# An attention and maxout FFN kernel: token tiles of 256 and 384 in place of 384 alone

## The chip, the core and the metric

The kernel runs on one core of one Trainium2 chip. The metric is the device time of one execution in microseconds (us). A core has five engines that run side by side, each through its own queue in order: PE (matrix multiply; its weight loads are shown apart as PEld), DVE (vector), ACT (activation), POOL (GpSimd) and SP, which here only issues DMAs. PE writes to PSUM banks; ACT and DVE read them, POOL can't.

## What is computed

Eight batches with eight heads, 576 tokens and 64 numbers per head. Half of the heads attend to the last 32 tokens, half to every fourth of the last 128. The result, turned to 4608 tokens of 512 numbers, goes through an FFN whose hidden layer is the elementwise largest of three products.

```python
scores = scale * np.matmul(q, k.transpose(0, 1, 3, 2))
mask_plain = (rel >= 0) & (rel < window)
mask_dil = (rel >= 0) & (rel < window * dilation) & (rel % dilation == 0)
...
attn = attn / (np.sum(attn, axis=-1, keepdims=True) + 1e-09)
return np.matmul(attn, v).astype(np.float32)
...
h = np.maximum(np.maximum(x @ w1, x @ w2), x @ w3)
return (h @ w_out).astype(np.float32)
```

## The kernel before

**Units.** The attention is cut into 64 units: a unit is half of a batch's tokens (288, the constant HALF) for two heads, and four units make one half (NPAIR). The first twelve units (LEAN) are written by dense (L490): scores s (L498 to L530, on PE with a mask added by a matmul), the largest value and the exponentials (DVE, ACT), the sums, the division W (norm, L595, mostly on POOL), transposes pt on PE, copies PT by ACT or DVE, and the product with the values, pv (L612). The other 52 are written by attention and behind (L650, L683), which turn W with transposes of DVE instead of PE. At the end of each unit, rounded (L638) writes the sum xH, a rounded part, and xL, the rest, into a ring of 1152 tokens (RING, four halves).

**Weights.** Each of the 36 weight pieces (24 of the three up matrices, 12 of the down matrix) is loaded as 64-bit floating-point numbers and made into two 32-bit parts by a chain in weight (L382): two first steps (rebias on ACT, low3 on POOL), two integer steps on DVE (joined, sign), the high part (split, wupH or wdn) on ACT, and the low part (wupL or wdn) on POOL. Four up pieces c serve one of the six column groups f (NF); two down pieces serve one wdn tile.

**FFN.** ffn (L803) takes a tile of n tokens that starts at token t0. For each of the six f and each of the three matrices g, twelve matmuls of n columns (three terms of four, L815) gather in one of two PSUM banks (the tag ffn in BANKS); DVE or ACT takes the bank out into tmp, ACT rounds it to h, POOL subtracts for the low part of h. Then, for each 128 tokens of the tile, 18 matmuls of 512 columns (down, L870) make a block d of the output, which ACT copies to o and SP sends away. A chain named prev keeps all FFN matmuls in the order in which the program lists them: all u of a tile, all d of it, then the next tile.

**What a tile asks for.** In the loop at L930 a tile of n tokens from t0 may begin when every half with a token below t0 + n is there:

```python
halves = range(t0 // HALF, -(-(t0 + n) // HALF))
...
*(x_of[h, p][xz] for h in halves for p in range(NPAIR)),
*(w_of[4 * f + c][wz] for c in range(4)),
```

**Order.** Nothing is issued as it is listed. A planner (class Plan, L96) holds all steps with estimated costs per engine, gives each a goal and a due time that is worked back from the FFN's matmuls (deadlines, L122), and goes through time, taking at each point the step that can begin first (order, L157). Steps with several possible engines may spill to another one. Before the first FFN matmul, it puts filler matmuls (idle, L951) into PE's gaps, and a run of 16 where its clock passes 21 and 35 us (BURSTS). The order is thus fixed when the program is built, and each engine works through its queue in that order and waits where something is missing.

Of the kernel before, what the change touches and what calls it, by code (L numbers as in the profile page):

```python
# [25 lines left out]
NEG = -8e9  # L26
REBIAS = 2.0**-112
TICK = 10.24 / 3
TILES = [384] * 12


LEAN = 12
# [235 lines left out]
def tile_dilated_window_attention__then__maxout_ffn(  # L268
# [660 lines left out]
    u = t0 = 0  # L929
    for n in TILES:  # L930
        plan.kind = "a"
# [81 lines left out]
```

## Time and profile before

| | |
|---|---|
| median of 3 runs | 736.94 us (736.81 to 736.97) |
| span of the profiled execution, first to last instruction | 734.8 us |
| busy PE, weight loads, DVE, ACT, POOL | 721.2, 661.3, 379.7, 305.4, 237.3 us |
| granted clock of PE, mean | 0.999 |
| first FFN matmul; first d matmul | 49.15; 100.72 us |
| filler matmuls | 72, all before 49.15 us |

The profile is that of one execution; its time outside the span isn't shown, and the median stands 2.1 us above the span. A view of groups gives, for each line and shape, the count, the busy time, the mean duration of one, and the idle time of the engine ahead of it with what ended it. The chain of waits follows back from the last instruction to what released each step. A busy PE is not PE at its peak: matmuls overlap, so the pace is read from how long a run of them lasts, divided by their count.

### The profile page before, as it was taken

What the parts mean: (1) busy time and instruction counts of PE and PEld (TensorE: products, weight loads), DVE (VectorE), ACT (ScalarE), POOL (GpSimd) and SP (SyncE); (2) the same over time, 40 slices, a digit from 0 to 9 for tenths busy, and PEclk for the clock granted to TensorE, in tenths of its full rate; (3) what the DMA queues carried; (4) which work ended last, traced back from release to release, by engine and by line L of the source; (5) the groups of instructions that cost most, each with busy time, mean ns of one, the idle gap of its engine ahead of it and who ended that gap; (6) DMA issues with size and microseconds to landing.
All of it is one profiled execution on the core that took longest, in us unless ns stands there. A gap on an engine that the chain in (4) does not pass through costs nothing.

```text
span 734.8 us, 14338 instructions
## 1 busy us (share of the span) xinstructions
PE 721.2 (98%) x5212; PEld 661.3 (90%) x5212; DVE 379.7 (52%) x1479; ACT 305.4 (42%) x1149; POOL 237.3 (32%) x359
## 2 busy tenths in 40 slices
PE   7899999999999999999999999999999999999998
PEld 4568889999998998998998999999999899998996
DVE  5999874565655554665555555555454461011110
ACT  4877754344444444343435343444442441111111
POOL 3798842322331321332222233233221131011110
PEclk9999999999999999999999999999999999999999
DMA  9973522122113123212212302212220100100001
GB/s 314 313 225 114 186 72 71 44 78 85 64 57 106 57 64 99 64 58 92 67 51 68 100 24 63 88 57 78 85 65 22 68 2 1 43 1 29 15 0 44
DMA packets 32103, 57.55 MB, mean 78 GB/s; under 512 B 3104, under 2 KB 11296, under 8 KB 32032
## 3 DMA queue, kind: packets, MB, share of 16 engines
q1 hardware_dynamic: 32032, 56.64, 24.1%
q8 instruction: 41, 0.67, 0.4%
q14 instruction: 30, 0.25, 0.1%
HBM read 47.19 MB, written 9.44 MB: 77 GB/s over the span
## 4 chain that ended last, share of the span: by engine, by line
PE 87%; DVE 5%; POOL 3%; issue 2%; ACT 1%; DMA 1%; POOLq 0%; DVEq 0%; ACTq 0%
PE u L817 57%; PE d L872 20%; PE s L670 5%; PE pv L776 4%; DVE cp L435 1%; DVE c L443 1%; POOL W L359 1%; DVE mx L538 1%; POOL wupL L359 1%; DVE W L359 1%; DMA k<-in_qk_d_dram 1%; POOL c L431 1%; ACT W L563 0%; DVE sm L583 0%; PE idle L951 0%
## 5 line engine op out<-in xcount | busy, mean ns | idle before, releaser
L359 DVE TENSOR_TENSOR tmp<-u,tmp 128x384 f32<-128x384 f32 x144 | 80.2, 557 | 207.7 <-PE u L817 201.6
L817 PE MATMUL u<-xH,wupH 128*128 128x384 f32 x864 | 185.8, 336 | 0.0
L817 PE MATMUL u<-xH,wupL 128*128 128x384 f32 x864 | 185.6, 335 | 0.0
L817 PE MATMUL u<-xL,wupH 128*128 128x384 f32 x864 | 185.4, 335 | 0.0
L359 POOL TENSOR_TENSOR h<-tmp,h 128x384 fp32r<-128x384 f32 x72 | 72.9, 1012 | 255.5 <-ACT h L352 255.4
L817 PEld LDWEIGHTS u<-xH,wupH 128*128 128x128 f32 x864 | 152.6, 188 | 2.0
L817 PEld LDWEIGHTS u<-xH,wupL 128*128 128x128 f32 x864 | 152.3, 188 | 0.8
L817 PEld LDWEIGHTS u<-xL,wupH 128*128 128x128 f32 x864 | 152.4, 188 | 0.7
L872 PE MATMUL d<-wdn,h 128*128 128x512 f32 x648 | 152.2, 392 | 0.5 <-DVE tmp L359 0.5
L693 ACT ACTIVATE W<-W,mx 96x128 f32<-96x128 f32 (+3 forms) x364 | 134.6, 372 | 38.1 <-DVE mx L702 37.4
L764 DVE STREAM_TRANSPOSE PT<-W 32x192 f32<-32x192 f32 (+1 forms) x312 | 125.0, 401 | 38.4 <-POOL W L359 34.2
L872 PEld LDWEIGHTS d<-wdn,h 128*128 128x128 f32 x648 | 120.7, 188 | 26.4 <-DVE tmp L359 0.8
L352 ACT CAST h<-tmp 128x384 fp32r<-128x384 f32 x72 | 36.9, 513 | 192.2 <-DVE tmp L359 192.2
L359 POOL TENSOR_TENSOR W<-W,sm 96x384 f32<-96x384 f32 (+3 forms) x125 | 99.7, 812 | 51.7 <-DVE sm L743 43.2
L702 DVE CUSTOM_DVE_ANT_0 W<-s,masks 96x128 f32<-96x128 f32 (+3 forms) x364 | 71.5, 256 | 59.6 <-PE s L670 59.6
L693 ACT ACTIVATION_READ_ACCUMULATOR W<-W,mx 72x1 f32 (+1 forms) x364 | 68.7, 189 | 0.0
L738 POOL TENSOR_TENSOR sm<-sm,small_c 96x6 f32<-96x6 f32 (+1 forms) x52 | 10.3, 198 | 164.5 <-ACT W L693 164.4
L352 ACT COPY tmp<-u 128x384 f32<-128x384 f32 x72 | 34.5, 479 | 51.2 <-PE u L817 51.1
L352 ACT COPY o<-d 128x512 f32<-128x512 f32 x36 | 21.1, 587 | 81.3 <-PE d L872 81.3
L670 PE MATMUL s<-k 64*96 64x128 f32 (+3 forms) x728 | 38.7, 254 | 0.0
L352 ACT CAST xH<-pv 128x288 fp32r<-128x288 f32 x51 | 19.7, 397 | 42.1 <-PE pv L776 35.2
L670 PEld LDWEIGHTS s<-k 64*72 64x72 f32 (+1 forms) x728 | 33.7, 149 | 2.7 <-issue 0.2
(56 smaller groups left out, 428.2 us busy)
## 6 DMA issues: line engine op xcount, KB each, us to landing
k<-in_qk_d_dram SPq DMA_DIRECT2D x32, 352.0 KB
k<-in_qk_p_dram SPq DMA_DIRECT2D x32, 304.0 KB
st<-in_w_up_dram SPq DMA_DIRECT2D x24, 384.0 KB
out_dram<-o SPq DMA_DIRECT2D x36, 256.0 KB
v<-in_v_d_dram SPq DMA_DIRECT2D x32, 208.0 KB
v<-in_v_p_dram SPq DMA_DIRECT2D x32, 192.0 KB
st<-in_w_dn_dram SPq DMA_DIRECT2D x12, 256.0 KB
```

The costliest lines, as they stand in the source:

```text
L352: nc.scalar.copy(dst, src)
L359: (nc.vector if eng == "dve" else nc.gpsimd).tensor_tensor(dst, a, b, op=op)
L431: (nc.gpsimd if e == "pool" else nc.vector).tensor_scalar(cw(), b, 1 / 32, -31 / 64, ALU.mult, ALU.add)
L435: nc.vector.scalar_tensor_tensor(pw(), pw(), 3, cw(), op0=ALU.logical_shift_left, op1=ALU.bitwise_or)
L670: nc.tensor.matmul(banks[j].t[:nq, wk * i : wk * i + nk], kb.t[d, q0 : q0 + nq], kb.t[d, k0 : k0 + nk], start=True, stop=True,)
L693: nc.scalar.activation(a, a, AF.Exp, bias=mx.t[:nq, n : n + 1], scale=-1.0, accum_out=sm.t[:nq, n : n + 1])
L702: nc.vector.tensor_tensor_reduce(W3()[:nq, n, mo : mo + nk], banks[j].t[:nq, wk * i : wk * i + nk], mask[:nq, mo : mo + nk], -0.125, 3e38, ...
L738: nc.gpsimd.tensor_tensor(a, a, eps_c[:nq].broadcast_to([nq, 2 * nb]), op=ALU.add)
L764: nc.vector.transpose(PT.t[c : c + 32, : 2 * nb, 32 * i : 32 * i + 32], W3(e)[32 * i : 32 * i + 32, :, c - e : c - e + 32],)
L776: nc.tensor.matmul(pv.t[64 * j : 64 * j + 64, q0 : q0 + nq], v.t[:wk, j, i, :], PT.t[:wk, nb * j + i, :nq], start=True, stop=True,)
L817: nc.tensor.matmul(bank.t[:, :n], wt[:, 3 * f + g, c, :], (xL if xz else xH)[:, c, r0 : r0 + n], start=(m == 0 and c == 0), stop=(m == 2 a ...
L872: nc.tensor.matmul(bank.t, hs[f].t[:, hz, s0 : s0 + 128], wdn[f].t[:, wz], start=(f == 0 and m == 0), stop=(f == NF - 1 and m == 2),)
```

## The change

The list of token tiles is other. Everything else is the same text.

```diff
-TILES = [384] * 12
+TILES = [256] * 3 + [384] * 10
```

Thirteen tiles in place of twelve: tokens 0 to 767 go as three tiles of 256, the other 3840 as ten of 384. None crosses the end of the ring (256, 512, 768, 1152). The matmuls of u go from 2592 to 2808 (216 for each tile, whatever its width); those of d stay 648. The first tile asks for half 0, units 0 to 3, where it asked for halves 0 and 1; the second for halves 0 and 1, the third for 1 and 2, the fourth for 2 and 3. Since the planner works back from the FFN, every engine's order changes. The names below are those of the program: s scores, pt transposes, pv the product with the values, u and d the FFN's banks (u0_5_2 is token 0, f 5, g 2; d0_128 is the tile at token 0, its second block of 128), and the last number is a running one.

On PE, at the start of the FFN, before:

```order
L615 MATMUL pv7_743<-PT1_1_87,v7_637 64x72 x8
...
L520 MATMUL s9_0_761<-k9_376 96x128
L520 MATMUL s9_1_762<-k9_376 96x128
L817 MATMUL u0_0_0_781<-xH_71,wupH_69 128x384 x4
L817 MATMUL u0_0_0_781<-xL_72,wupH_69 128x384 x4
L817 MATMUL u0_0_0_781<-xH_71,wupL_70 128x384 x4
```

And with the change:

```order
L615 MATMUL pv3_530<-PT1_1_87,v3_316 64x72 x8
...
L520 MATMUL s6_0_546<-k6_225 72x104
L520 MATMUL s6_1_547<-k6_225 72x104
L817 MATMUL u0_0_0_567<-xH_71,wupH_69 128x256 x4
...
L817 MATMUL u0_0_0_567<-xL_72,wupH_69 128x256 x4
L817 MATMUL u0_0_0_567<-xH_71,wupL_70 128x256 x4
```

The first u stood behind pv of unit 7 and the scores of unit 9; it now stands behind pv of unit 3 and the scores of unit 6. The fillers ahead of it go from 72 to 62. The transposes and pv of units 4 to 7 and the scores of units 7 to 9 come after it.

On PE, where tile 0 goes from its last u to what follows, before:

```order
L817 MATMUL u0_5_1_1443<-xL_72,wupH_69 128x384 x4
L615 MATMUL pv11_1460<-PT1_1_87,v11_1419 64x72 x8
L817 MATMUL u0_5_1_1443<-xH_71,wupL_70 128x384 x4
L817 MATMUL u0_5_2_1485<-xH_71,wupH_69 128x384 x4
L817 MATMUL u0_5_2_1485<-xL_72,wupH_69 128x384 x4
L817 MATMUL u0_5_2_1485<-xH_71,wupL_70 128x384 x4
L872 MATMUL d0_0_1504<-wdn0_1146,h0_0_928 128x512 x3
L872 MATMUL d0_0_1504<-wdn1_1183,h0_1_1021 128x512 x3
```

And with the change, from the last piece of the first block of d to the first u of the second tile:

```order
L872 MATMUL d0_0_1235<-wdn5_1361,h0_5_1227 128x512 x3
L872 MATMUL d0_128_1437<-wdn0_1054,h0_0_693 128x512 x3
L601 MATMUL pt10_1_1447<-ident_66,W_2_82 104x72 x4
L601 MATMUL pt11_0_1456<-ident_66,W_3_83 104x72 x4
L601 MATMUL pt11_1_1466<-ident_66,W_3_83 104x72 x4
L872 MATMUL d0_128_1437<-wdn1_1128,h0_1_774 128x512 x3
L615 MATMUL pv10_1480<-PT1_0_86,v10_1239 64x72 x8
L615 MATMUL pv11_1491<-PT1_1_87,v11_1363 64x72 x8
L872 MATMUL d0_128_1437<-wdn2_1206,h0_2_867 128x512 x3
...
L872 MATMUL d0_128_1437<-wdn5_1361,h0_5_1227 128x512 x3
L817 MATMUL u256_0_0_1527<-xH_71,wupH_69 128x256 x4
```

pv of unit 11 stood among the last u of tile 0, ahead of all d. Now it stands inside the second of the two blocks of d, twelve d matmuls ahead of the first u of the second tile; the scores of units 12 and 13 come ahead of it as before.

On POOL, at the end of the weights, before:

```order
L359 TENSOR_TENSOR wdn4_1383<-c32_1352,wdn4_1383 128x256
L431 TENSOR_SCALAR c34_1410<-st34_1363 128x256
L738 TENSOR_TENSOR sm12_1204<-sm12_1204,small_c_73 96x6
L431 TENSOR_SCALAR c35_1423<-st35_1380 128x256
L359 TENSOR_TENSOR wdn4_1383<-c33_1393,wdn4_1383 128x256
L359 TENSOR_TENSOR W_1_81<-W_1_81,sm12_1204 96x384
L359 TENSOR_TENSOR h0_4_1440<-tmp0_4_1365,h0_4_1440 128x384
L359 TENSOR_TENSOR wdn5_1450<-c34_1410,wdn5_1450 128x256
L359 TENSOR_TENSOR wdn5_1450<-c35_1423,wdn5_1450 128x256
```

And with the change:

```order
L359 TENSOR_TENSOR wdn4_1322<-c32_1296,wdn4_1322 128x256
L431 TENSOR_SCALAR c34_1343<-st34_1301 128x256
L359 TENSOR_TENSOR wdn4_1322<-c33_1310,wdn4_1322 128x256
L431 TENSOR_SCALAR c35_1353<-st35_1316 128x256
L359 TENSOR_TENSOR wdn5_1361<-c34_1343,wdn5_1361 128x256
L359 TENSOR_TENSOR wdn5_1361<-c35_1353,wdn5_1361 128x256
L359 TENSOR_TENSOR W_2_82<-W_2_82,sm10_1305 96x416 x2
L359 TENSOR_TENSOR W_3_83<-W_3_83,sm11_1405 96x416 x2
L738 TENSOR_TENSOR sm12_1431<-sm12_1431,small_c_73 96x6
```

The divisions W of units 10 and 11 stood about 20 rows ahead of the last wdn; now they are the last of POOL's work for the dense units, behind the last wdn.

## The prediction

> **What bounds the kernel now.** First the page: the span, the busy shares, and the 40 slices.
>
> ```profile
> span 734.8 us, 14338 instructions
> PE   7899999999999999999999999999999999999998
> DVE  5999874565655554665555555555454461011110
> POOL 3798842322331321332222233233221131011110
> PEclk9999999999999999999999999999999999999999
> ```
>
> PE is busy in nearly every slice at full clock, while DVE and POOL are full only in the first five or six, about 100 us. So there are two stages. The chain of waits, in order of time, says where the second begins, and what tiles cost in it.
>
> ```profile
> 100.72 4.43 PE d L872 x18
> ...
> 669.30 12.29 PE d L872 x54
> 681.59 37.45 PE u L817 x216
> 719.03 12.30 PE d L872 x54
> 731.35 0.59 ACT o L352
> ```
>
> A tile of 384 is 37.45 us of u and 12.29 us of d: 37.45 / 216 = 173.4 ns for a matmul of 384 columns, 12.29 / 54 = 227.6 ns for one of 512. From 100.72 us, where the first d of tile 0 begins, the chain is almost PE alone. The windows show the same, and what the first stage looks like.
>
> ```profile
> 0.00:25.00 25.00, 20.95 (x169) 11.91 (x170) 17.05 (x47) 14.59 (x58) 11.27 (x27) 1.00 0.94 335
> 25.00:50.00 25.00, 21.88 (x233) 13.81 (x232) 22.76 (x53) 19.45 (x57) 22.92 (x29) 1.00 0.75 230
> 50.00:75.00 25.00, 23.41 (x166) 21.47 (x165) 24.34 (x50) 18.76 (x62) 22.13 (x30) 1.00 0.48 153
> 75.00:100.70 25.70, 24.39 (x193) 22.32 (x191) 22.07 (x72) 18.55 (x63) 21.33 (x33) 1.00 0.45 141
> 100.70:731.40 630.70, 630.59 (x4456) 591.76 (x4456) 293.44 (x1260) 233.55 (x912) 159.62 (x242) 1.00 0.18 57
> ```
>
> The columns after the length are PE, PEld, DVE, ACT, POOL. Behind 100.7 PE has no gap (630.59 of 630.70): that stage is the sum of its matmuls. Ahead of it DVE and POOL are at about nine tenths, with the weights and the dense units. PE begins the FFN in the middle of that:
>
> ```profile
> 49.15 0.97 PE L817 MATMUL u<-xH,wupH 128*128 128x384 f32 x4
> ...
> L951 PE MATMUL idle<-masks,identb 128*128 128x512 bf16 x72 | 19.2, 404 | 3.0 <-DVE masks L345 3.0
> ```
>
> Up to 49.15 us it waits or runs 72 fillers (19.2 us); from there to 100.7 it runs tile 0's u.
>
> **The second stage: what the narrow tiles cost.** 384 columns at 2.4 per ns (the granted clock is 0.999) would stream in 160 ns, 512 in 213.3; the two measured paces lie 13.4 and 14.3 ns above. A matmul of 256 columns isn't in the trace. The straight line through 384 and 512 gives 173.4 - 128 x 0.423 = 119.2, the stream of 106.7 and the same 13.4 give 120.1; I take 120. A narrow tile's u is then 216 x 120 = 25.9 us where two thirds of 37.45 would be 25.0: 0.9 us lost per narrow tile, because the number of matmuls doesn't fall with the width. The bounds: 109.5, if the cost above the stream were only that of the fillers,
>
> ```profile
> 36.43 3.63 PE L951 MATMUL idle<-masks,identb 128*128 128x512 bf16 x16
> L817 PEld LDWEIGHTS u<-xH,wupH 128*128 128x128 f32 x864 | 152.6, 188 | 2.0
> 165.87 1.15 PE pv L776 x32
> ```
>
> whose 16 take 3.63 us, or 216 ns each once the last one's own length of 0.4 us is set apart; and 173, if the weight load binds. One load lasts 188 ns and the next starts 173 ns later, so they overlap already, by 15 ns here; in pv 32 matmuls with their own loads pass in 1.15 us, 36 ns each, so loads can follow much more closely. I stay near the line, the nearest rows.
>
> The Trainium skill ("TensorE: Matmul & The Clock Gate", section "Back-to-back issue gap") gives N / 2.4 + 2.5 ns for an isolated warm matmul: an estimate of 109.2 for 256 columns, with which the two narrow tiles below would cost 4.7 us less. The traces put 384 and 512 columns 11 ns and more above that rule (173.4 against 162.5), so I don't take it. Its section "LDWEIGHTS (loading the stationary operand)" gives 107 ns for 128 columns of weights, as long as the narrow matmul itself: an estimate by which the load would just be covered. No run here shows that yet.
>
> **The first stage: when tile 0 is done.** With 256 tokens the first u no longer waits for units 4 to 7 and starts sooner; u0 is also shorter. But the order in which it stands shows what comes next: the two blocks d0_0 and d0_128 stand ahead of the second tile, and pv of units 10 and 11 stand inside the second. So u256, from which PE can run on, waits for all of wdn and all of the dense units, as d did before. I call its start T. d0_0's last piece waits for wdn5; queued behind it on PE are pt10, pt11, d0_128 and u256, and ACT, DVE and SP wait for those in turn, but none of them is late for anything before T.
>
> POOL makes the last of both (wdn5, then W of units 10 and 11). Its rows in that stage before:
>
> ```profile
> L359 POOL TENSOR_TENSOR wupL<-c,wupH 128x384 fp32r<-128x384 f32 x24 | 24.0, 1011 | 2.0 <-ACT wupH L352 1.1
> L431 POOL TENSOR_SCALAR c<-st 128x384 uint32<-128x384 uint8 x20 | 10.8, 540 | 1.6
> L359 POOL TENSOR_TENSOR W<-W,sm 96x416 f32<-96x416 f32 x11 | 9.6, 877 | 1.1 <-DVE sm L586 0.9
> L359 POOL TENSOR_TENSOR wdn<-c,wdn 128x256 fp32r<-128x256 f32 x12 | 9.0, 761 | 0.7 <-ACT wdn L352 0.4
> L359 POOL TENSOR_TENSOR W<-W,sm 96x384 f32<-96x384 f32 x8 | 6.6, 840 | 2.0 <-DVE sm L586 1.6 <-DVE sm L743 0.2
> L359 POOL TENSOR_TENSOR h<-tmp,h 128x384 fp32r<-128x384 f32 x5 | 5.1, 1011 | 0.1
> L431 POOL TENSOR_SCALAR c<-st 128x256 uint32<-128x256 uint8 x12 | 5.0, 419 | 1.5 <-DMA st<-in_w_dn_dram 0.5
> ...
> 20.90:98.60 77.70, 72.16 (x615) 58.64 (x611) 71.23 (x181) 60.16 (x196) 68.73 (x94) 1.00 0.60 190
> POOL W L359 <- DVE sm L586: 2.5, 2, 1.6
> POOL wupL L359 <- ACT wupH L352: 1.1, 1, 1.1
> ```
>
> Both orders agree on POOL up to W of unit 2, which ends at 20.9 us; the last wdn ended at 98.6. In these 77.7 us POOL was busy for 68.7; of the other 9.0, waits are 4.7 (the two rows above and three small ones), the rest are pauses between steps. With the change I count from the same point to W of unit 11: 23 wupL, 18 c of 384, 10 W of 416, 8 of 384, 12 c of 256, 12 wdn, and 6 h, now of 256 columns, for which I take the 0.75 of wdn, the same operation of that width. By the rows' busy time over their count that is 23.0 + 9.7 + 8.7 + 6.6 + 5.0 + 9.0 + 4.5 = 66.5 us. With the same 9.0 beside it W of unit 11 ends at 96.4 us; with no wait at 91.7. Behind it stand pt, PT and pv of unit 11, and twelve d matmuls at 227.6 ns, 2.7 us:
>
> ```profile
> 44.89 0.46 PE L601 MATMUL pt<-ident,W 72*104 72x72 f32 x4 [0.16 <-POOL W L359]
> 45.39 0.40 ACT L352 COPY PT<-pt 104x288 f32<-104x288 f32 x1
> 47.22 0.72 PE L615 MATMUL pv<-PT,v 104*64 104x72 f32 x16
> ```
>
> 0.46 + 0.40 + 0.72 = 1.6. So POOL puts T between 96.0 and 100.7. DVE gives a second answer: from xL of unit 0 (20.4) to xL of unit 11 (100.2) it was busy for 73.1 us. Of its rows there the change drops six transposes of unit 12 (0.37 each in the chain of waits, 2.2), two W that POOL has now (1.93), and about half a us of copies and evictions, 4.6 us in all; with its gaps as before it would reach xL of unit 11 at 95.6, pv about 1.2 earlier, and T at 97.1.
>
> ```profile
> 20.40:100.20 79.80, 73.13 (x185) 1.00 0.59 188
> 95.42 1.93 DVE W L359
> ...
> 99.35 0.37 DVE PT L764
> ```
>
> I take **T = 98**, between POOL's two ends and near DVE's. PE isn't the one to wait for: it begins earlier by four units, and u0 and two blocks of d are 25.9 + 8.2 = 34.1 us where 37.45 were.
>
> **The sum.** Before, PE had left at 100.7 us eleven u of 37.45 and 36 blocks of d; at T it has two u of 25.9, ten of 37.45, and 34 blocks of 4.1 (a third of 12.29). The attention left is the same, scores of units 12 and 13 being done in both. 51.8 + 374.5 - 411.95 = +14.35, less 8.2: **+6.15 us** of work that remains. The span becomes 734.8 + (98 - 100.7) + 6.15 = 738.25, 3.45 more. Those 3.45 are put on the median, which stands 2.1 above the span and holds the same head and tail: **740.4 us**. That is: the FFN starts earlier, but the stage with POOL and DVE ends only 2.7 us earlier, with 4.25 us less of FFN (37.45 against 25.0 + 8.2) behind it, and two narrow tiles then cost 1.9.
>
> **The rivals.** *The first stage ends much sooner* (faster). If POOL loses its waits, since PE and the dense units no longer come late together, and its pauses too, W of unit 11 ends at 20.9 + 66.5 = 87.4 and T is 91.7: 734.8 - 9.0 + 6.15, or 734.1 by the median. It decides below T = 93, where the gain passes 1.5 us. For it: all the waits are on steps in front of or beside POOL, which move. Against: its pauses between dependent steps stay. I give it 0.14.
>
> *Even.* T from 93 to 96 gives 735.5 to 738.4; 0.16. Narrow matmuls at 109.5, with no more above the stream than the fillers have, take 432 x 10.5 ns = 4.5 us off two tiles: 735.9, even too; 0.04, since both widths in the trace lie 13 to 14 ns above the stream. (That pace is the rule of the Trainium skill named above.)
>
> *Narrow tiles stall PE* (slower still). The two PSUM banks come round in 12 x 120 = 1.44 us where it was 2.08, and an eviction by DVE takes 557 ns at 384:
>
> ```profile
> L359 DVE TENSOR_TENSOR tmp<-u,tmp 128x384 f32<-128x384 f32 x144 | 80.2, 557 | 207.7 <-PE u L817 201.6
> ```
>
> Where DVE has a row of other work ahead of it, PE waits; DVE idles for 201.6 us waiting for u, so mostly there is room. It would cost 1 to 3 us in two tiles: 741.5 to 743.5. 0.10.
>
> *The weight load binds*, at up to 173 ns: 53 ns on 432 matmuls are 23 us, 763 us. pv's rows speak against it. 0.03.
>
> The forecast itself, T from 96 to 101, has 0.53: 738.4 to 743.4.
>
> **Range and chances.** About 0.2%, 1.5 us, is what a measurement of this kernel tells from no change. From the cases: faster 0.14, same 0.20, slower 0.66. The range 735.2 to 745.0 takes in T from 93 to 102 with some stall, and leaves out most of the first rival and the weight load.
>
> **What would show it.** Right: the first u at about 35 to 40 us, PE with waits for POOL's W and wdn between 70 and 98, u256 beginning at 96 to 101 with no wait behind it, and a run of 216 matmuls of 256 columns near 25.9 us. Wrong: u256 before 94 (POOL had less to wait for), u of 256 at 24 us or less, or waits of PE behind u256.

## The result, and the profile after

The changed kernel takes **742.23 us** (741.53 to 742.97, 4 runs) beside 736.96 (736.81 to 737.32, 4 runs): a ratio of 1.007, 95% interval 1.0058 to 1.0083. It is slower, by 5.3 us; forecast were 3.5. The span of the profiled execution is 740.3 us, 5.5 more than before. First the page:

```profile
span 740.3 us, 14788 instructions
PE   7999799999999999999999999999999999999998
PEclk9999899999999999999999999999999999999999
```

New is the fifth slice (74 to 92.5 us): PE is at 7 there instead of 9, and its clock at 8. The chain of waits, whose columns are start, duration and step, from the last units of the first stage on and at its end:

```profile
77.30 4.35 DMA st<-in_w_dn_dram
...
86.53 0.73 POOL wdn L359
87.31 1.22 PE d L872 x2
88.53 1.16 PE pv L615 x12
89.69 2.58 PE s L670 x24
...
95.48 0.75 PE d L872 x3
96.23 1.15 PE pv L615 x32
97.38 2.99 PE d L872 x12
100.37 8.63 PE u L817 x72
...
724.50 12.30 PE d L872 x54
736.82 0.59 ACT o L352
```

T, the start of u256, is 100.37 us. From there the chain runs to 736.82, 636.45 us; before it ran from 100.72 to 731.35, 630.63. So the second stage holds 5.8 us more (forecast 6.15) and begins 0.35 us sooner (forecast 2.7). The u row behind T has 8.63 / 72 = 119.9 ns per matmul of 256 columns. And the windows (columns as before):

```profile
75.00:100.40 25.40, 20.97 (x180) 15.73 (x181) 17.32 (x65) 18.82 (x70) 17.50 (x27) 0.87 0.56 166
100.40:736.80 636.40, 636.38 (x4636) 599.24 (x4634) 298.01 (x1277) 236.81 (x925) 161.84 (x248) 1.00 0.18 56
```

Behind T PE has no gap, with 180 matmuls more than before (216 more of u, 36 fewer of d). The 25 us ahead of T are where the forecast gain is missing: PE is busy for 20.97 of 25.4 there, 24.39 of 25.7 before, at a clock of 0.87. The timelines of POOL and PE, and behind them the windows of that place, say why:

```profile
80.51 0.41 POOL L431 TENSOR_SCALAR c<-st 128x256 uint32<-128x256 uint8 x1 [1.01 <-DMA st<-in_w_dn_dram]
...
92.46 1.72 POOL L359 TENSOR_TENSOR W<-W,sm 96x416 f32<-96x416 f32 x2 [0.86 <-DVE sm L586]
...
83.64 0.44 PE L601 MATMUL pt<-ident,W 96*128 96x96 f32 x3 [3.21 <-POOL c L431]
...
84.00:86.00 2.00, 1.80 (x9) 1.03 (x7) 2.00 (x5) 1.74 (x9) 1.94 (x3) 0.77 0.55 149
86.00:88.00 2.00, 1.22 (x4) 0.52 (x3) 1.21 (x4) 1.60 (x8) 1.68 (x4) 0.50 0.38 98
88.00:90.00 2.00, 2.00 (x18) 1.32 (x18) 0.93 (x4) 1.41 (x6) 1.42 (x3) 0.50 0.36 107
90.00:92.00 2.00, 2.00 (x23) 2.00 (x22) 1.83 (x7) 1.02 (x3) 1.60 (x2) 0.52 0.00 0
92.00:94.00 2.00, 2.00 (x26) 1.62 (x23) 0.90 (x7) 1.04 (x4) 1.54 (x2) 1.00 0.55 156
```

A piece of the down weights lands late, and POOL waits 1.01 us for it. PE's transposes wait for a division W that stands behind that piece in POOL's queue, 3.21 us in all. (That W ends at 83.15, half a us before PE goes on. What holds PE in the half us isn't settled: the view names POOL's c, which the transposes don't read.) The granted clock (third number from the right) is then about half from 85.1 to 91.9 us. In that time 24 scores take 2.58 us. W of unit 11, the last of POOL's work that T needs, ends at 92.46 + 1.72 = 94.18 us, and POOL had stood idle for 0.86 us ahead of it.

### The profile page after: what moved, and what is told of

Its sections match the earlier page's. It is cut to its first block, busy times and chain, and to the rows that moved or that the text cites. A ratio compares the mean times of both kernels' runs of the same rounds, so it can differ in the third digit from the quotient of the medians.

```text
span 740.3 us, 14788 instructions
## 1 busy us (share of the span) xinstructions
PE 725.0 (98%) x5418; PEld 665.4 (90%) x5418; DVE 378.1 (51%) x1490; ACT 309.3 (42%) x1163; POOL 238.3 (32%) x364
## 4 chain that ended last, share of the span: by engine, by line
PE 89%; POOL 3%; DVE 3%; issue 2%; DMA 1%; ACT 1%; DVEq 0%; POOLq 0%; SPq 0%; ACTq 0%
PE u L817 58%; PE d L872 20%; PE s L670 5%; PE pv L776 4%; DMA st<-in_w_up_dram 1%; POOL W L359 1%; POOL wupL L359 1%; POOL c L431 1%; DVE c L443 1%; DVE mx L538 1%; DMA st<-in_w_dn_dram 1%; DVE cp L435 0%; ACT W L563 0%; PE idle L951 0%; PE pv L615 0%
## 5 line engine op out<-in xcount | busy, mean ns | idle before, releaser
L817 PE MATMUL u<-xH,wupH 128*128 128x384 f32 (+1 forms) x936 | 190.4, 324 | 0.6 <-ACT tmp L352 0.6
L359 DVE TENSOR_TENSOR tmp<-u,tmp 128x384 f32<-128x384 f32 (+1 forms) x156 | 82.2, 527 | 209.9 <-PE u L817 202.1
L817 PE MATMUL u<-xH,wupL 128*128 128x384 f32 (+1 forms) x936 | 189.1, 323 | 0.0
L817 PE MATMUL u<-xL,wupH 128*128 128x384 f32 (+1 forms) x936 | 188.9, 323 | 0.0
L817 PEld LDWEIGHTS u<-xH,wupH 128*128 128x128 f32 x936 | 156.7, 188 | 3.4 <-ACT tmp L352 0.8
L359 POOL TENSOR_TENSOR h<-tmp,h 128x384 fp32r<-128x384 f32 (+1 forms) x78 | 74.1, 950 | 259.7 <-ACT h L352 259.4
L817 PEld LDWEIGHTS u<-xH,wupL 128*128 128x128 f32 x936 | 156.9, 189 | 0.6
L817 PEld LDWEIGHTS u<-xL,wupH 128*128 128x128 f32 x936 | 157.0, 189 | 0.4
L352 ACT CAST h<-tmp 128x384 fp32r<-128x384 f32 (+1 forms) x78 | 38.1, 489 | 204.0 <-DVE tmp L359 204.0
L352 ACT COPY tmp<-u 128x384 f32<-128x384 f32 (+1 forms) x78 | 35.6, 456 | 53.9 <-PE u L817 52.4
```

The lines of the kernel that those rows point to most:

```text
L352: nc.scalar.copy(dst, src)
L359: (nc.vector if eng == "dve" else nc.gpsimd).tensor_tensor(dst, a, b, op=op)
L817: nc.tensor.matmul(bank.t[:, :n], wt[:, 3 * f + g, c, :], (xL if xz else xH)[:, c, r0 : r0 + n], start=(m == 0 and c == 0), stop=(m == 2 a ...
```

## The experiments

T is in each case the start of u of the second tile. Since PE has next to no gap behind T, a kernel with the same work behind it shows its T in its span, us for us: in the changed kernel and the seven runs below that keep its tiles and its twelve dense units, the last copy o begins 636.37 to 636.45 us after T. The medians come from four rounds, in which the kernel before had 736.53 to 737.53 us, so a difference of less than a us between medians of two rounds isn't read here. Each ratio is to the kernel before in the same round.

### The price of a narrow tile

The three narrow tiles at the end instead of the start, so that the first stage is that of before:

```diff
-TILES = [256] * 3 + [384] * 10
+TILES = [384] * 10 + [256] * 3
```

> The ten tiles of 384 first, the three of 256 last: the order of the first 100 us is that of the kernel before. If a narrow tile costs only the fixed part of its matmuls, each u of 256 takes 25.9 us (216 x 120 ns), the three cost 3 x 25.9 - 2 x 37.45 = 2.8 us, and the time is 736.95 + 2.8 = 739.8, with no wait of PE in them. If narrow tiles stall PE in other ways (two banks that come round sooner), it is over 741. If all of the change's 5.3 us come from the first stage, it is 737.

740.15 us, ratio 1.0042 (1.0027 to 1.0057), span 737.7, 2.9 more than before. The end of its chain:

```profile
100.77 4.39 PE d L872 x18
...
700.08 25.91 PE u L817 x216
725.99 8.22 PE d L872 x36
```

The first d stands at 100.77, where it stood before (100.72), and each narrow tile has 25.91 us of u, 119.95 ns for a matmul. Three times 0.94 lost (25.91 against two thirds of 37.45) are 2.8 of the 2.9 us: with the first stage untouched, the narrow matmuls' fixed cost is all there is in the profiled execution. The medians of the round lie 3.6 us apart (740.15 and 736.53), and the runs of each are spread over about 3 us; the 0.7 us between isn't explained.

Narrower still, two tiles of 256 and 128 tokens instead of the first of 384:

```diff
-TILES = [256] * 3 + [384] * 10
+TILES = [256, 128] + [384] * 11
```

> Tiles of 256 and 128 tokens, then eleven of 384. A matmul of 128 columns streams in 53 ns. If the pace is the stream and 13.4 ns, as for 256, 384 and 512 columns: the 216 u matmuls of the tile of 128 pass in 14.4 us, and the second stage (the work that remains behind T) is within 0.5 us of the changed kernel's, 742-744 with the same T. If the weight load (one each 107-111 ns) binds below 256 columns: 23-24 us, some 9 us more, 750-753. Between the two: the load's pace.

753.99 us, ratio 1.0228 (1.0212 to 1.0244). The row of the 128-wide u in its chain:

```profile
103.77 14.24 PE u L817 x128
```

That is 111.25 ns for each, 24.0 us for 216, where the stream of 128 columns and 13.4 ns would be 67 ns. The stretch from T to the last copy o is 9.7 us longer than in the changed kernel, as expected for a bound by the weight load; T itself, 103.77, is 3.4 us later, which puts the time above the 750 to 753 that were given for the same T. The forecast's rival "the weight load binds" is thus real in kind, but lies below 256 columns: a matmul of u, with 128 columns of weights of its own, doesn't come in under 111 ns here, and at 119.9 the tile of 256 is 8.7 ns clear of it. That the load is what sets the 111 ns is likely, and not shown by itself: the loads have next to no gap there (14.17 of 14.24 us busy), but neither has PE. The Trainium skill ("TensorE: Matmul & The Clock Gate", section "LDWEIGHTS (loading the stationary operand)") gives 107 ns for 128 columns of weights; this run lies 4 ns above that.

### Is the early start worth anything?

The first tile asks for halves 0 and 1 again; all else as in the changed kernel:

```diff
-        halves = range(t0 // HALF, -(-(t0 + n) // HALF))
+        halves = range(t0 // HALF, max(2, -(-(t0 + n) // HALF)))
...
-        while HALF * (u // NPAIR) < t0 + n:
+        while HALF * (u // NPAIR) < max(t0 + n, HALF + 1):
```

> The change, but the first tile of 256 waits for halves 0 and 1, as the first tile of 384 did: the first u at 49 instead of 36. If the first stage is bound by POOL and DVE, the early start is worth little: the second tile begins at 100 to 103 (100.4 with the change), 742 to 745. If PE's early start does shorten the stage, it begins 5 us later or more: over 747.

748.03 us, ratio 1.0138 (1.0113 to 1.0162). Its chain at T:

```profile
100.33 6.45 PE d L872 x21
106.78 4.79 PE u L817 x40
```

T is 106.78, 6.4 us later than in the changed kernel, and the time lies over the 747 that stood for an early start that shortens the stage. With the early start T is back at 100.4, where the kernel before was with its first d, and no further. But the planner's whole order is other in this run: ahead of T PE waits for a load of v that lands at 98.96, behind the last wdn, and the clock is at half from 96.5 to 103.4 us. How much of the 6.4 us is the start alone isn't separated.

### A fourth buffer for the output

```diff
-        "o": (3, [128, DM], F32),
+        "o": (4, [128, DM], F32),
```

> The change with a fourth buffer o, through which the pieces of the down matrix are loaded. In the profile of the change PE waits 3.2 us at 80 to 84 us, behind POOL's wait for such a piece, and its granted clock is about half from 84 to 92. If the loads are late for want of a buffer, they come earlier, that wait falls below 2 us, the clock stays full, the second tile begins at 97 to 98 instead of 100.4, and the time is 739 to 740. If the loads are late for another reason (SP's queue, the wire), the wait and the halved clock stay: 742.

742.56 us, ratio 1.0068 (1.0048 to 1.0089), T 100.79. Neither case came true as it was put. The order of the first stage came out other, so the buffer alone isn't tested: the wait of 3.2 us is gone (the longest of PE's waits from 79 to 89 us is 1.09 us), but the clock is at half from 88.4 to 95.2 us all the same, and T hardly moved. It is an early hint that T doesn't hang on one wait, nor the clock on one long wait.

### What the halved clock costs

Fourteen matmuls of zeros are added to the first block of d, which leaves the sums as they are and fills PE's wait:

```diff
+    zerob = const.tile([128, 128], BF16, name="zerob")
+    nc.gpsimd.memset(zerob, 0.0)
...
+                    if t0 == 0 and s0 == 0 and f == 2:
+                        for _ in range(14):
+                            nc.tensor.matmul(bank.t, zerob, masks.rearrange("p n k -> p (n k)"), start=False, stop=False)
```

> The change with 14 matmuls of zero weights added into the first d bank, 3.0 us of PE work where it waited 3.2 us: no other order, no other wait. If the halved clock behind that wait is what made the first stage end later than forecast, the clock stays full, the scores of units 12 and 13 take 1.5 us instead of 2.6, the second tile begins at about 98 instead of 100.4, and the time is about 739.8. If POOL's last division alone sets that start, it stays at 100 and the time at 742.

740.59 us, ratio 1.0047 (1.0031 to 1.0062). The window 88 to 92 us, and the chain (lines from 300 on are two higher):

```profile
88.00:92.00 4.00, 3.81 (x56) 3.25 (x56) 2.87 (x11) 2.86 (x10) 3.10 (x4) 1.00 0.46 119
...
89.03 1.48 PE s L672 x24
...
92.43 1.72 POOL W L361 x2
94.19 0.46 PE pt L603 x4
94.65 0.74 PE d L874 x3
95.39 1.15 PE pv L617 x32
96.54 2.99 PE d L874 x12
99.53 8.63 PE u L819 x72
```

The clock stays at 1.00, and the same 24 scores take 1.48 us instead of 2.58. But T falls only from 100.37 to 99.53, by 0.84 us where about 2.4 were expected: PE now runs into POOL's W of unit 11, which ends at 94.14, as it did in the changed kernel (94.18). So the wait took the place of the slow clock. The end of that W isn't POOL's count alone: POOL stands idle just ahead of it in both runs (0.86 and 0.74 us), and W begins 0.16 to 0.17 us after DVE's reciprocal of that unit has ended, at 92.29 and 92.26. The chain also gives the path from W of unit 11 to T at full clock, 5.4 us: 0.46 + 0.74 + 1.15 + 2.99, and a joint of 0.05. The forecast had 4.3 (1.6 + 2.7).

### Which engine sets T

Two runs each take 13.7 us of work from one engine between 20 and 94 us, with the order left as it is. (The 13.7 are a sum of durations, and records on one engine overlap a little: from 20.5 to 94.2 us the busy time falls by 12.9 us on POOL, from 66.14 to 53.23, and by 9.5 on DVE, from 64.39 to 54.89.) The first takes it from POOL:

```diff
-                tt(e, W3(j, j + 1), W3(j, j + 1), m, ALU.mult)
+                if not 4 <= u < LEAN:
+                    tt(e, W3(j, j + 1), W3(j, j + 1), m, ALU.mult)
```

> The changed kernel, but with the 16 divisions W of units 4 to 11 left out (those units are not divided by their sums); the order of everything else is the same. That takes 16 x 0.86 = 13.7 us of work from POOL between 20 and 94 us, where POOL was busy for 65.8 of 73.7 us. If POOL's count sets T, the start of u256, as the prediction had it: T falls from 100.4 by 6 us or more, to 88-94, and the time by as much, to 730-736. If DVE's work sets it and POOL only stands beside it: T falls by less than 2 us, to 98.5-100, 740-742. Between, T 95-98: both share it.

739.28 us, ratio 1.0029 (1.0019 to 1.004); T 97.30. The second takes it from DVE (the sign step in weight):

```diff
-            nc.vector.scalar_tensor_tensor(
+            if j < 8:
+              nc.vector.scalar_tensor_tensor(
```

> The changed kernel, but with the sign step on DVE (L443) left out for weight pieces 8 to 35 (those weights lose their sign); the order of everything else is the same. That takes 28 x 0.49 = 13.7 us of work from DVE between 20 and 94 us, as much as the run without divisions takes from POOL. If POOL's count sets T: T falls by less than 2 us, 98.5-100, 740-742. If DVE's work sets it: T falls by 6 us or more, to 88-94, 730-736. Between: both share it.

742.55 us, ratio 1.0069 (1.0053 to 1.0086); T 100.34. So T stands still with less work on DVE, but the chain (its lines from 443 on are one higher) shows two changes that cancel:

```profile
86.50 1.22 PE d L873 x2
...
88.88 2.81 PE s L671 x24
...
100.34 8.63 PE u L818 x72
```

PE's last stretch without a gap begins 0.81 us sooner than in the changed kernel (87.31) and lasts 0.78 us longer (13.84 against 13.06): the clock is at half for 10.24 us here, from 82.6 to 92.9, where it was for 6.83. W of unit 11 ends at 93.37, 0.81 us sooner. With the 5.4 us of path behind it, an estimate of T at full clock is 98.8, against the 99.53 of the run with zeros; no run shows it. DVE's work alone is thus worth little, but not shown to be worth nothing.

POOL's is worth 3.1 us, though 13.7 were taken, and W of unit 11 itself left the path with them: T was bound by POOL, but another bound lies just behind. The chain of the run without divisions shows which (its lines from 600 on are one higher, those of the next two runs up to three):

```profile
79.39 3.15 DMA st<-in_w_dn_dram
...
83.19 0.74 POOL wdn L359
83.97 1.22 PE d L873 x2
...
86.39 2.81 PE s L671 x24
...
94.31 2.99 PE d L873 x12
97.30 8.63 PE u L818 x72
```

POOL now has time, but waits for the down weights, and from 83.97 PE works off its queue to T without a gap, 13.3 us, part of it at half clock. SP's queue shows what the loads wait for (total, times, longest), in the run without divisions:

```profile
SPq L449 <- DVE c L443: 23.0, 15, 3.7
SPq L476 <- PE s L520: 13.1, 6, 8.2
```

L449 is the load of st, which waits until DVE's sign step gives a buffer st free; L476 is the load of k, which stands between them and waits for PE's scores. Both guesses were put to a run. The first leaves out the divisions and the sign step together (the two diffs above):

> Both at once: the divisions of units 4 to 11 (13.7 us of POOL) and the sign step of weight pieces 8 to 35 (13.7 us of DVE) left out, the order the same. The sign step alone left T at 100.3, the divisions alone brought it to 97.3, with the last pieces of the down weights landing at 79 to 82.5 us in both. If those loads come late because DVE frees the st buffers late (SP waited 23.0 us for the sign step of the run without divisions): the loads come 3 us or more sooner, PE starts its last queue sooner, T 91-95, 731-736. If PE's own queue and the loads of k and v that stand between them on SP hold it: T 96.5-97.5, 738.5-740.

737.44 us, ratio 0.9995 (0.9983 to 1.0007), T 95.02:

```profile
73.71 4.50 DMA st<-in_w_dn_dram
...
81.72 0.74 POOL wdn L359
82.51 1.22 PE d L874 x2
...
95.02 8.63 PE u L819 x72
```

The sign step, whose loss left T as it was in the run above, moves T by 2.28 us where POOL has been relieved. Of these, 1.46 are PE's earlier start on its last queue (82.51 against 83.97); 0.82 are that queue, 12.5 us instead of 13.3, since the half clock ends at 86.0 us instead of 89.1. SP issues the last load of the down weights at 78.8 us instead of 80.6, so 1.8 us sooner, less than the 3 us and more that I expected; T lies at the upper end of what was given. DVE acting on T through the buffers st and SP's queue fits this. But the sign step also stands in each piece's own chain, which is 0.4 us shorter without it, and the two aren't separated. One of the ten executions kept a mean clock of 0.999 and took 735.14 us; the other nine, at 0.995, took 737.06 to 738.19: the half clock is worth about 2 us here too. The other run leaves out the divisions and adds the zero matmuls:

> The run without divisions, with the 14 matmuls of zeros put into PE's wait ahead of the first block of d, as in the run with zeros (nothing is added to the sums). Without divisions PE had work without a gap from 83.97 to T at 97.30, 13.3 us, of it about 4.7 us at half clock. If PE's queue sets T there and the zeros keep the clock up: T falls by 2.0 to 2.5 us, to 94.8-95.3, 736.5-738. If something else stands just behind it, as POOL's W of unit 11 did in the run with zeros (0.84 us gained): T 96.3-97.3, 738.5-740.

737.80 us, ratio 1.0001 (0.9991 to 1.0011), T 95.84:

```profile
82.63 2.76 DMA v<-in_v_p_dram
85.53 0.72 PE pv L618 x12
...
95.84 8.63 PE u L820 x72
```

T falls by 1.46 us, between the two expectations: from that pv on the queue takes 10.3 us, where the run without divisions has 12.1 at the slower clock (97.30 less the end of its d, 83.97 and 1.22); but pv now waits for a load of v, and starts 0.3 us later than there.

| run | what differs | T, us | time, us |
|---|---|---|---|
| changed kernel | | 100.37 | 742.23 |
| without sign | DVE -13.7 us | 100.34 | 742.55 |
| zero matmuls | full clock | 99.53 | 740.59 |
| without division | POOL -13.7 us | 97.30 | 739.28 |
| no division, zero matmuls | full clock, POOL | 95.84 | 737.80 |
| no division, no sign | POOL and DVE | 95.02 | 737.44 |

No engine alone holds T. POOL's count, the landing of the down weights (by st buffers and SP's order), and PE's queue behind them at a halved clock stand close behind one another: freeing one moves T by 0 to 3.1 us (the 0 with a longer half clock against it), two by 4.5 to 5.4, and then the next one holds it.

### The planner's constants chosen anew

If the order is what wastes the early start, another order may use it. The constants were chosen anew for these tiles by the planner's own estimate:

```diff
-LEAN = 12
+LEAN = 8
-STAGE, STAGE_H = ["wd", "h", "wd"], 16
+STAGE, STAGE_H = ["wd", "h", "wd"], 24
-SPILL = 2.088
+SPILL = 1.079
-FFN_PACE = 1.044
-UNIT_PACE, UNIT_SLACK, UNIT_LEAD = 1.271, 7.676, 3.484
+FFN_PACE = 1.829
+UNIT_PACE, UNIT_SLACK, UNIT_LEAD = 0.917, 9.33, 4.677
-WEIGHT_PACE, WEIGHT_SLACK, WEIGHT_LEAD = 0.3, 2.817, 0.8
+WEIGHT_PACE, WEIGHT_SLACK, WEIGHT_LEAD = 0.3, 2.817, 1.481
-        "o": (3, [128, DM], F32),
+        "o": (4, [128, DM], F32),
```

> The changed kernel with the planner's constants chosen anew for these tiles: eight dense units instead of twelve (LEAN), other paces and due times, wd/h stage for 24 pieces, four o buffers. By the planner's own costs the program ends 6 us sooner than the changed kernel (2.5 us sooner than the kernel before). If those costs hold on the chip: T near 94.5, 735-737, equal to or below the kernel before. If the waits that the plan doesn't know (a DMA that comes late, a halved clock) take it back: T 97-101, 738-743. The narrow tiles' own 1.9 us stay in either case.

738.89 us, ratio 1.0019 (1.0009 to 1.0028): 3.3 us better than the changed kernel, and still a little behind the kernel before. A line of its chain, and its groups of attention matmuls behind T (count, busy us, mean ns, idle before):

```profile
90.19 6.71 PE u L817 x56
...
L670 PE MATMUL s<-k 64*96 64x128 f32 (+3 forms) x760 | 40.0, 253 | 0.0
L776 PE MATMUL pv<-PT,v 104*64 104x72 f32 (+1 forms) x784 | 34.5, 238 | 0.4 <-DVE PT L764 0.3
```

T is 90.19, ten us sooner, lower than I had allowed for. But its last d ends at 733.65, 643.5 us later, 7.0 more than in the changed kernel: with eight dense units instead of twelve, 56 more scores and 56 more pv stand behind T (704 and 728 in the changed kernel). At the paces of the chains (24 scores in 1.48 us, 32 pv in 1.15) that is 3.5 + 2.0 us; of the other 1.5, 0.8 are gaps of PE (642.69 of 643.46 us busy), and the rest was not traced further. Work that is taken from the first stage comes back in the second.

## Why the prediction came out as it did

The forecast of slower held, and 742.23 lies in the range, which was made for T up to 102; it is 1.8 us above the 740.4 named. That is more than half of the 3.45 forecast; T alone came 2.4 us late. The first u stands at 36.46 us, within the 35 to 40 named. By its steps:

**The narrow tile's cost: right.** 120 ns taken, 119.9 measured, 119.95 in three narrow tiles at the end. The isolated-matmul rule of the Trainium skill (109.2, named in the prediction) would have been 10.7 ns too low. What the 13 ns above the stream are, no run here tells. (The fillers' pace is 215 ns by its row, 3.63 less 0.40 over 15, not 216; that moves only the lower bound, by 1 ns.)

**The work behind T: right.** +6.15 forecast, +5.8 measured. The 0.33 between are the first block of d in the kernel before, 4.43 us where a third of 12.29 was taken.

**T: the steps it waits for were named, the size was wrong.** 98 taken, 100.37 measured. Its terms:

- POOL's count: right in size. 66.5 us of work and W of unit 11 between 91.7 and 96.4 were forecast; POOL was busy for 65.8 us and W ended at 94.18, its last wait one for DVE's reciprocal. But this W didn't set T in the changed kernel: PE came to the transposes behind it only after 94.7 us. It did in the run with zeros.
- The path from there to T: mis-sized. "Behind it stand pt, PT and pv of unit 11, and twelve d matmuls" gave 4.3 us. The run with zeros has 5.4 at full clock: pv of unit 10 and three d of piece f 1 stand in that path too, and the twelve d took 2.99 us, not 2.7. The first two can be read in the rows of PE's order shown under the change, and I left them out.
- The halved clock: not foreseen, 0.84 us. At full clock the path ends at 94.14 + 5.4, 99.53 us; with the half clock PE's own queue ends 0.84 later, at 100.37.
- "PE isn't the one to wait for" fell. PE worked without a gap from 87.31 to T, 13.06 us: pv, scores, transposes and d had gathered behind the wait for wdn.
- DVE's answer, 97.1, isn't borne out either: with 13.7 us taken from DVE T was 100.34, and 98.8 by the estimate at full clock, still above 97.1. So DVE's count isn't what holds T; its steps reach T through POOL's last W, which waits for its reciprocal, and, as it seems, through the loads that wait for its buffers.

**The rivals.** "The first stage ends much sooner" took POOL's count for the one bound. T at 95 was reached only with 13.7 us taken from both POOL and DVE, and its T of 91.7 in no order with twelve dense units. Narrow tiles don't stall PE: 636.38 of 636.40 us are busy. *The weight load binds* came true at 128 columns, with 111 ns instead of the 173 feared, and not at 256. The rows of pv (36 ns) were no argument against it: their loads have 64 columns.

## What to carry to other kernels

Where the count of matmuls doesn't fall with the width of a tile, a narrower tile pays their fixed time once more: price an early start by that, and by the work that must now be done ahead of the steady stage, before counting the microseconds by which the first matmul moves. Count the whole queue of the engine that ends the stage, row by row, behind the step it waits for. Where several engines are nine tenths busy up to the same moment, take work from one alone and little may move; the runs that take from two show what each is worth. An end that doesn't move isn't yet no effect: look whether the clock moved the other way.

## What the runs showed of the hardware

After a wait of 3.21 us PE's granted clock was about half from 85.1 to 91.9 us (windows of 84 to 92 us: 0.77, 0.50, 0.50, 0.52); with 13 zero matmuls recorded in the wait it stayed at 1.00. In the profiled execution of the kernel before, the windows of this stage show 1.00.

One long wait isn't needed: with the fourth buffer o the clock fell though PE's longest wait in the ten us ahead of it was 1.09 us. Eight of the profiled executions have such a fall. The half clock lasted 6.83 us in six of them, 10.24 in the run without sign and 13.66 in that with the tile of 128, which are two, three and four times 3.41. If each of the eight is divided into steps of 3.41 us counted from its own fall, all read alike from about 10 to 100 us. In the step that ends with the fall PE was busy for 1.0 to 1.8 us, and in every other step at full clock for 2.0 us or more. The full clock came back at the end of the first step that PE filled without a gap; steps at half clock in which it was busy for 2.1 to 3.2 us didn't bring it back.

The Trainium skill ("TensorE: Matmul & The Clock Gate", section "What's actually happening") gives an idle window of about 3.4 us for the fall to half; here a step of that length with up to 1.8 us of work in it was enough. It also has a busy window of that length for the return, and each return here stands at the end of one.

What the half clock costs depends on who is late: 0.84 us where POOL came next, 1.46 where the loads did.
